# Idle matmuls of 512 columns, two memsets for eleven, and a branch placed three products later

## The chip, the cores and the metric

One Trainium2 chip, one of its cores. The metric is the device time of one execution in microseconds, the median of the runs.

## The reference

The kernel computes two layers in one launch. The first is an attention whose keys and values are mixed between blocks by a matrix that five Sinkhorn steps make from `sort_net`; the second is a gated feed-forward layer with a spatial product over the 768 tokens.

```python
# P: (4, 8, 8, 8), five times: exp(P - max), divided by row sums, then by column sums
k_sorted = einsum('bhij,bhjcd->bhicd', P, k_blocks)      # 8 blocks of 96 tokens
v_sorted = einsum('bhij,bhjcd->bhicd', P, v_blocks)
attn = softmax(q_block @ k_sorted_block.T / 8)           # within each block
x = (attn @ v_sorted_block)                              # -> (4, 768, 512)

h = maximum(x @ w_in, 0)                                 # (4, 768, 1024)
u, v = h[..., :512], h[..., 512:]
v_n = (v - mean(v)) / sqrt(var(v) + 1e-6)
v_s = einsum('ts,bsd->btd', w_spatial, v_n) + b_spatial[None, :, None]
out = (u * v_s) @ w_out                                  # (4, 768, 512) float32
```

q, k and v are (4, 8, 768, 64) float32. The kernel multiplies in bfloat16 and sums in float32.

## The kernel before

The order of all work is written by hand. The string `ORDER` is a list of short items, and each names a function `u_...` with its arguments: `SC:2:1:3:1` is the score product with its exp in PSUM tile 2 for batch 1, head pair 3, half 1. The items are issued in this order; each engine takes its own instructions from the list and waits only for the semaphores that the recording layer derives from the tiles it reads and writes. There are four PSUM tiles of two banks, `ps0` to `ps3`, and each item names the one that it uses.

The work goes over the four batches. For each one: q is turned (`QT`, `QQ`), k is mixed and turned in one product (`KT`), v is mixed (`VT` and `VB` for the first batch, `VM` and `VC` later), scores and exps per half (`SC`), product with v and division (`AT`), turning of x (`XT`, `XD`), the second half of `w_in` (`VP`), statistics (`ST`, `LN`, `LA`), the first half (`UP`), the spatial product (`SP`, `GT`) and the output product (`OP`, `OE`, `OS`). The batches overlap in the list. Loads of q, k, v and the weights are issued on GpSimd (`L`), most stores on SyncE.

The items that the change and the prediction speak of:

- `CO` (`u_CO`) clears `warm`, `eps` and `ones` and then the pads of the exp buffers `ex` (five) and of the turned k buffers `kt` (six), all on VectorE. The pads are the 32 columns behind the data, which 128-column weight loads read beyond a block of 96.
- `DM` (`u_DM`, L226) issues matmuls on the zero tile `warm` whose results nobody reads; they keep TensorE busy at the start. `DM:0:12:256` is twelve of 256 columns into `ps0`. Six groups stand before the first mixing of k: three of twelve by 256, then three of six by 512.
- `SK` (L238 to L251) is a Sinkhorn step, an exp on ScalarE and seven short VectorE operations. Its first exp waits for the load of `sort_net`.
- `QT` (L314) turns q of the first batch on TensorE after ScalarE has cast it (`QC`).
- `KT` and `VT` (L383) mix k and v of the first batch; `VT` needs the load `v_in`.
- `SH` (L666) is the spatial product of the last batch in pieces of 512 and 256 tokens, with the addition on VectorE (L672), and `GH` (L679) the gating.
- `OH` (L686) is an output product of the last batch, four matmuls over a token tile and a column range; `OI` copies it from PSUM (L115 on ScalarE, L117 on VectorE), and `OJ` stores it (L698). There are eight such products: `OH:1:3:2` and `OH:2:3:3` of 512 columns, `OH:0:3:4` and `OH:3:3:5` of 256, `OH:2:3:5` of 256, `OH:1:3:1` of 512, `OH:3:3:4` of 256, and last `OH:2:3:0` of 512.
- `IF` is the place of a branch (L794). A flag that the kernel has computed on the way (`CK`, `CF`, `LF`) says whether the fast arithmetic without maxima stayed in range; each engine reads it into a register. The items behind `IF` are the usual branch, and the alternative does the whole computation again in a safe way. Every engine resolves the branch in its own sequencer. `BH` marks the branch as likely taken for TensorE, VectorE and ScalarE. Before the change `IF` stands ahead of all eight output products.

Of the kernel before, what the change touches and what calls it, by code (L numbers as in the profile page):

```python
# [16 lines left out]

ORDER = """
IV:0 CO S0 SK:0 SK:1 LH:S:0 L:q:0:4:8 L:k:0:0:8 L:v:0:0:8 SK:2 IV:2 ID MA L:v:1:0:8 MC QC:A:1 SK:3 L:k:1:0:8 MB QC:A:0
DM:0:12:256 L:q:1:0:8 DM:2:12:256 DM:1:12:256 QT:3:A:0:1 SK:4 QT:2:A:0:3 DM:0:6:512 DM:3:6:512 L:wv QT:1:A:0:0  # L20
QT:2:A:0:2 PR:0 P0:0:2 L:wu P0:6:8 P0:2:4 DM:3:6:512 P0:4:6 PC:D KT:1:D:0:1 PD:1:4:8 KT:3:A:0:0 L:wsb L:wsa KT:0:D:0:3
KT:2:A:0:2 IV:1 L:v:2:0:8 VT:1:A:0:0 VT:3:D:0:1 PD:1:0:4 SC:0:0:0:0 SC:2:0:0:1 VB:1:D:0:0 L:k:2:0:8 VB:3:D:0:1
SC:0:0:1:0 VT:1:A:0:2 AT:2:0:0:0 VT:3:A:0:3 PD:2:4:8 AT:0:0:1:0 L:q:2:0:8 VM:1:A:1:0 VB:2:D:0:2 SC:3:0:1:1
XT:0:D:0:0:0 AT:1:0:0:1 SC:2:0:2:0 VM:3:A:1:3 VB:0:D:0:3 PD:2:0:4 SC:1:0:2:1 AT:2:0:2:0 KT:3:D:1:1 KT:0:D:1:2
SC:1:0:3:0 VM:2:A:1:1 SC:3:0:3:1 AT:1:0:1:1 KT:2:A:1:3 KT:0:A:1:0 AT:3:0:3:0 VM:1:A:1:2 PD:3:4:8 QQ:2:D:1:0
XT:3:D:0:1:0 L:k:3:0:8 AT:0:0:3:1 XT:1:A:0:0:2 QQ:2:A:1:2 AT:3:0:2:1 VP:1:A:0:0:1 XT:0:D:0:1:2 ST:0:1 VP:2:D:0:2
ST:0:0 SC:0:1:1:1 SC:3:1:2:1 L:q:3:0:8 VC:1:4:8 VP:1:D:0:4:5 SC:2:1:3:1 ST:0:4 ST:0:5 SC:3:1:3:0 VP:0:A:0:3 SC:2:1:0:1
ST:0:2 UP:1:A:0:1:1 AT:0:1:1:1 L:v:3:0:8 SC:3:1:0:0 ST:0:3 UP:2:A:0:0:0 AT:0:1:3:1 AT:1:1:2:1 LN:0:0:6 UP:3:A:0:0:1
AT:0:1:0:1 LA:0:5 WW:2:A:0 WW:1:D:4 XT:3:A:1:1:2 UP:0:A:0:1:0 LA:0:2 VC:1:0:4 AT:2:1:0:0 VM:1:A:2:1 BI WW:3:D:2
SC:0:1:2:0 VM:2:A:2:2 XT:1:D:1:1:0 LA:0:0 BH LA:0:4 LA:0:1 LA:0:3 VM:3:A:2:0 SC:0:1:1:0 VP:1:A:1:4:5 AT:2:1:3:0  # L30
AT:0:1:1:0 ST:1:5 SP:3:0:2 AT:0:1:2:0 L:wo SP:1:0:0 VM:2:D:2:3 SP:0:0:1 VC:2:4:8 XT:3:D:1:0:2 XT:1:A:1:0:0 VC:2:0:4
QQ:2:D:2:0 KT:0:A:2:1 KT:3:D:2:0 GT:D:0:0 QQ:1:D:2:2 KT:2:A:2:2 KT:0:A:2:3 PD:3:0:4 GT:P:0:2 VP:3:A:1:0:1 SC:1:2:0:1
SC:2:2:0:0 SP:0:0:3 ST:1:4 SC:3:2:2:1 SC:1:2:1:1 ST:1:1 VP:2:A:1:2:3 KT:3:D:3:2 QQ:0:D:3:0 ST:1:2 SC:1:2:3:0
UP:2:A:1:1:0 AT:0:2:0:1 GT:P:0:3 KT:3:A:3:0 ST:1:3 QQ:1:D:3:2 SC:0:2:3:1 AT:2:2:2:1 UP:3:D:1:0:1 VM:1:A:3:3
UP:0:A:1:0:0 AT:2:2:3:1 UP:3:A:1:1:1 GT:P:0:1 ST:1:0 LN:1:0:6 AT:2:2:1:1 AT:0:2:3:0 XD:2:1 LA:1:4 OP:1:0:0 AT:2:2:0:0
OE:A:0:0 OP:0:0:2 SC:2:2:2:0 LA:1:2 LA:1:5 OE:D:0:2 SC:1:2:1:0 LA:1:1 LA:1:0 LA:1:3 OP:3:0:4 AT:1:2:1:0 AT:0:2:2:0
SP:2:1:2 VM:0:D:3:1 VM:1:D:3:0 OE:A:0:4 VP:3:D:2:4:5 KT:0:A:3:1 KT:2:D:3:3 SP:1:1:3 VM:0:A:3:2 GT:D:1:3 OS:0:0 ST:2:4
SP:3:1:1 SC:2:3:3:1 SC:1:3:1:1 XD:2:0 OS:0:2 GT:D:1:2 ST:2:5 SP:0:1:0 VC:3:4:8 SC:3:3:2:1 SC:2:3:0:1 UP:1:D:2:1:0
GT:D:1:1 VC:3:0:4 VP:3:A:2:2:3 AT:1:3:3:1 GT:P:1:0 VP:2:A:2:0:1 ST:2:3 AT:1:3:2:1 AT:3:3:1:1 UP:0:A:2:1:1 OP:1:1:0
ST:2:0 ST:2:1 ST:2:2 OE:A:1:0 AT:2:3:0:1 LN:2:0:6 LA:2:1 UP:0:D:2:0:0 SC:1:3:0:0 LA:2:3 SC:3:3:1:0 LA:2:2 LA:2:5  # L40
LA:2:0 OP:2:1:4 AT:1:3:0:0 AT:3:3:1:0 XD:3:1 OE:A:1:4 OP:0:1:2 LA:2:4 SC:1:3:3:0 OE:D:1:2 SC:3:3:2:0 SP:2:2:2
AT:1:3:2:0 UP:0:A:2:0:1 AT:3:3:3:0 CK VP:2:A:3:4:5 GT:D:2:2 OS:1:2 SP:1:2:1 ST:3:5 OS:1:4 XD:3:0 SP:3:2:3 SP:2:2:0
ST:3:4 CF:3 GT:D:2:1 GT:P:2:3 UP:0:A:3:1:0 VP:2:D:3:2:3 VP:3:A:3:0:1 ST:3:0 ST:3:1 ST:3:2 UP:2:A:3:0:1 GT:P:2:0 LF
OP:1:2:2 ST:3:3 OE:A:2:2 LN:3:0:6 OP:0:2:0 LA:3:4 LA:3:5 OS:2:2 OE:A:2:0 UP:3:D:3:1:1 LA:3:2 LA:3:0 OP:2:2:4 LA:3:3
OE:A:2:4 LA:3:1 OS:2:4 UP:0:A:3:0:0 SH:1:3:3:0 GH:P:3:3:0 SH:2:3:0:0 GH:D:3:0:0 SH:0:3:1:0 SH:2:3:2:0 SH:3:3:1:1
GH:P:3:1:0 SH:1:3:0:1 GH:P:3:2:0 OS:1:0 GH:P:3:1:1 SH:2:3:3:1 SH:3:3:2:1 OS:2:0 GH:P:3:0:1 GH:D:3:2:1 GH:D:3:3:1
OS:0:4 IF OH:1:3:2:0:512:0:4 OH:2:3:3:0:512:0:4 OH:0:3:4:0:256:0:4 OI:A:3:2:0:512 OI:A:3:3:0:512 OH:3:3:5:0:256:0:4
OI:D:3:4:0:256 OI:D:3:5:0:256 OJ:3:2:0:512:S OJ:3:3:0:512:S OJ:3:4:0:256:S OJ:3:5:0:256:A OH:2:3:5:256:512:0:4
OH:1:3:1:0:512:0:4 OH:3:3:4:256:512:0:4 OI:D:3:5:256:512 OI:A:3:1:0:512 OJ:3:5:256:512:S OI:A:3:4:256:512
OJ:3:4:256:512:S OJ:3:1:0:512:A OH:2:3:0:0:512:0:4 OI:A:3:0:0:512 OJ:3:0:0:512:S  # L50
"""


# [12 lines left out]
def kernel(  # L66
# [131 lines left out]
    def u_CO():  # L198
        nc.vector.memset(warm, 0.0)  # L199
        nc.vector.memset(eps_tile, 1e-6)  # L200
        nc.vector.memset(ones, 1.0)
        for n in range(NE):
            nc.vector.memset(ex[n][:, 2 * NI * BLK:], 0.0)
        for n in range(NK):
            nc.vector.memset(kt[n][:, S:], 0.0)
# [622 lines left out]
```

## Time and profile before

| what | value |
|---|---|
| listed runs | 157.03, 157.03 and 158.32 us, median 157.03 us |
| profiled execution | 158.39 us, its span 156.6 us |
| granted TensorE clock in it | 0.989 of full speed (mean) |
| busy share of the span | TensorE 95%, VectorE 77%, ScalarE 52%, GpSimd 24% |
| chain that ended last | TensorE 84%, DMA 9%, ScalarE 2% |
| start of the branch | ScalarE 140.0, SyncE 142.9, TensorE 146.3, GpSimd 147.0, VectorE 148.4 us |

Rows are read as follows. A timeline row is: start, time, engine, line, operation, tile written and tile read, shape, count, and in brackets the idle time before it with what ended it. Rows of a chain are: start, time, engine and line. "q" behind an engine's name means its sequencer (ACTq), and PEld is TensorE's weight load, whose sequencer is PEldq. A matmul's time is from its start to its modelled end, so that neighbours overlap.

### The profile page before, as it was taken

To read this page: it belongs to the slowest core of one execution; us is meant where nothing else is said; L and a number is where in the kernel's file an instruction comes from. 1 tells how busy PE (TensorE), PEld (TensorE's weight loads), DVE (VectorE), ACT (ScalarE), POOL (GpSimd) and SP (SyncE) were. 2 spreads that over 40 slices of the span, in tenths; PEclk is the share of its full clock that TensorE was granted. 3 is DMA by queue.
4 is the path that set the end of the run, shared out by engine and by line. 5 is a ranking of instruction groups with operands and counts; after the bars stand their busy time and mean duration, and the time that the engine had idled before them with its cause. 6 is when DMAs were issued, how large, how long until landed. Compare 5 with 4: busy or idle time off the path is not lost.

```text
span 156.6 us, 4025 instructions
## 1 busy us (share of the span) xinstructions
PE 148.7 (95%) x1683; PEld 92.8 (59%) x1683; DVE 120.4 (77%) x270; ACT 81.8 (52%) x112; POOL 36.9 (24%) x43
## 2 busy tenths in 40 slices
...
PEclk9999879999999999999999999999999999999999
...
GB/s 80 262 203 205 203 205 205 206 211 234 255 240 205 204 205 204 230 208 4 0 4 234 10 229 43 153 14 4 100 107 199 66 0 0 110 51 375 148 218 186
DMA packets 27653, 23.57 MB, mean 151 GB/s; under 512 B 7280, under 2 KB 24688, under 8 KB 27632
## 3 DMA queue, kind: packets, MB, share of 16 engines
...
q10 hardware_dynamic: 288, 0.39, 0.7%
q8 instruction: 14, 0.23, 0.5%
...
HBM read 24.78 MB, written 6.29 MB: 198 GB/s over the span
## 4 chain that ended last, share of the span: by engine, by line
PE 84%; DMA 9%; ACT 2%; POOL 1%; DVE 1%; issue 1%; ACTq 0%; POOLq 0%
PE ps L609 15%; PE ps L597 14%; PE ps L554 14%; PE ps L636 10%; DMA v_in<-in_v_dram 9%; PE ps L488 5%; PE ps L666 5%; PE ps L442 4%; PE ps L383 4%; PE ps L686 3%; PE ps L314 3%; PE ps L410 2%; PE ps L518 2%; PE ps L401 1%; PE ps L531 1%; POOL q_in L169 1%
## 5 line engine op out<-in xcount | busy, mean ns | idle before, releaser
L447 ACT ACTIVATE ex<-ps 96x768 bf16<-96x768 f32 x32 | 24.8, 805 | 9.5 <-PE ps L442 9.5
L626 POOL TENSOR_TENSOR gt<-z,u_sb 128x768 bf16<-128x768 f32 x6 | 9.8, 1640 | 81.0 <-DVE z L615 61.2
L609 PE MATMUL ps<-wspT,v_sb 128*128 128x384 bf16 x144 | 25.1, 326 | 0.0
L597 PE MATMUL ps<-xT,w_in_sb 128*128 128x384 bf16 x128 | 23.5, 326 | 0.0
L496 DVE TENSOR_TENSOR x_sb<-ps,rec_all 96x512 bf16<-96x512 f32 x32 | 22.0, 686 | 1.1
L554 PE MATMUL ps<-w_in_sb,xT 128*128 128x512 bf16 x96 | 22.7, 380 | 0.0
L609 PEld LDWEIGHTS <-v_sb 128*128 128x128 bf16 x144 | 13.5, 98 | 8.9
L571 DVE BATCH_NORM_STATS2 stats<-v_sb 128x6 f32<-128x512 bf16 x24 | 16.3, 678 | 2.0 <-ACT v_sb L121 1.5
L115 ACT COPY o_sb<-ps 128x1024 f32<-128x1024 f32 (+2 forms) x12 | 9.7, 816 | 15.2 <-PE ps L686 10.2
L636 PE MATMUL ps<-w_out_sb,gt 128*128 128x512 bf16 x72 | 16.9, 379 | 0.0
L615 DVE TENSOR_TENSOR z<-ps,b_bc 128x768 f32<-128x768 f32 x12 | 11.4, 952 | 7.0 <-PE ps L609 6.8
L121 ACT ACTIVATE u_sb<-ps 128x768 bf16<-128x768 f32 x12 | 9.7, 810 | 13.1 <-PE ps L597 13.0
L597 PEld LDWEIGHTS <-w_in_sb 128*128 128x128 bf16 x128 | 11.6, 98 | 7.4
L554 PEld LDWEIGHTS <-xT 128*128 128x128 bf16 x96 | 8.7, 98 | 9.3
L121 ACT ACTIVATE v_sb<-ps 128x1024 bf16<-128x1024 f32 (+1 forms) x9 | 8.8, 976 | 8.7 <-PE ps L554 8.7
L488 PEld LDWEIGHTS <-ex 96*128 96x128 bf16 x256 | 10.7, 98 | 3.6 <-issue 0.2
L488 PE MATMUL ps<-vb,ex 96*128 96x65 bf16 x256 | 12.3, 195 | 0.0
L226 PE MATMUL ps<-warm 128*128 128x256 bf16 (+1 forms) x54 | 10.0, 353 | 1.3 <-DVE warm L199 1.3
L636 PEld LDWEIGHTS <-gt 128*128 128x128 bf16 x72 | 6.7, 98 | 7.2
L115 ACT CAST kt<-ps 128x768 bf16<-128x768 f32 x9 | 6.9, 800 | 6.5 <-PE ps L383 6.5
L442 PE MATMUL ps<-qT,kt 64*128 64x96 bf16 x256 | 9.4, 206 | 0.5 <-DVE kt L117 0.4
L442 PEld LDWEIGHTS <-kt 64*128 64x128 bf16 x256 | 6.3, 95 | 5.8 <-issue 3.9
...
## 6 DMA issues: line engine op xcount, KB each, us to landing
...
```

The lines of the kernel that those rows point to most:

```text
L115: nc.scalar.copy(out=out, in_=in_)
L121: nc.scalar.activation(out=out, in_=in_, func=AF.Relu)
L442: nc.tensor.matmul(t[:, hh, 0:HW].rearrange("p (g x) -> p g x", g=G)[:, :, ii * TB:(ii + 1) * TB], lhsT=kT[rows, i * BLK:i * BLK + 128], r ...
L447: nc.scalar.activation(out=e_tile(b, hp, ih).rearrange("p h (x g) -> p h x g", g=G), in_=t[0:BLK, :, 0:HW].rearrange("p h (g x) -> p h x g ...
L488: nc.tensor.matmul(t[:, hh, ii * VW:ii * VW + D + 1], lhsT=e[:, c:c + 128], rhs=vb[b % 2][:, ih * NI + ii, 2 * hp + hh, 0:D + 1], start=Tr ...
L496: nc.vector.tensor_mul(out=x_sb[:, hp].rearrange("p i (h d) -> p h i d", h=2), in0=tv[:, :, :, 0:D], in1=_raw_ap(rec, 0, [rec.ap[0], [NI, ...
L554: nc.tensor.matmul(t[:, x, :], lhsT=st["xT", b][:, n // 3, kc, (n % 3) * 128:(n % 3 + 1) * 128], rhs=w_in_sb[:, kc, DH:DFF], start=(kc == ...
L571: nc.vector.bn_stats(out=stats, in_=st["v_sb", b, n])
L597: nc.tensor.matmul(t[:, x, 0:HW], lhsT=w_in_sb[:, kc, mc * 128:(mc + 1) * 128], rhs=st["xT", b][:, ih, kc, :], start=(kc == 0), stop=(kc = ...
L609: nc.tensor.matmul(t[:, x, 0:HW], lhsT=st["v_sb", b, n][:, mc * 128:(mc + 1) * 128], rhs=wspT[:, 3 * x:3 * x + 3, n, :], start=(n == 0), s ...
L615: nc.vector.tensor_add(out=z.rearrange("p (x c) -> p x c", x=2), in0=t[:, :, 0:HW], in1=b_bc.rearrange("p (x c) -> p x c", x=2),)
L636: nc.tensor.matmul(t[:, x, :], lhsT=st["gt", b, mc][:, (n0 + x) * 128:(n0 + x + 1) * 128], rhs=w_out_sb[:, mc, :], start=(mc == 0), stop=( ...
```

## The change

Three edits. The first three groups of idle matmuls become six of 512 columns, so that all six groups are alike. The five `ex` buffers become slices of one tile `ex_all`, the six `kt` buffers slices of `kt_all`, and the pads of each are cleared by one memset over all slices. In `ORDER`, the first three output products `OH`, with their two copies on ScalarE and one on VectorE, stand ahead of `IF`; their stores stay behind it. The order among them is the same except that `OI:D:3:4` now comes before `OH:3:3:5`, on another engine than that one.

```diff
-DM:0:12:256 L:q:1:0:8 DM:2:12:256 DM:1:12:256 QT:3:A:0:1 SK:4 QT:2:A:0:3 DM:0:6:512 DM:3:6:512 L:wv QT:1:A:0:0
+DM:0:6:512 L:q:1:0:8 DM:2:6:512 DM:1:6:512 QT:3:A:0:1 SK:4 QT:2:A:0:3 DM:0:6:512 DM:3:6:512 L:wv QT:1:A:0:0 QT:2:A:0:2
...
-OS:0:4 IF OH:1:3:2:0:512:0:4 OH:2:3:3:0:512:0:4 OH:0:3:4:0:256:0:4 OI:A:3:2:0:512 OI:A:3:3:0:512 OH:3:3:5:0:256:0:4
-OI:D:3:4:0:256 OI:D:3:5:0:256 OJ:3:2:0:512:S OJ:3:3:0:512:S OJ:3:4:0:256:S OJ:3:5:0:256:A OH:2:3:5:256:512:0:4
+GH:P:3:1:1 SH:2:3:3:1 SH:3:3:2:1 OS:2:0 GH:P:3:0:1 GH:D:3:2:1 GH:D:3:3:1 OS:0:4 OH:1:3:2:0:512:0:4 OH:2:3:3:0:512:0:4
+OH:0:3:4:0:256:0:4 OI:A:3:2:0:512 OI:A:3:3:0:512 OI:D:3:4:0:256 IF OH:3:3:5:0:256:0:4 OI:D:3:5:0:256 OJ:3:2:0:512:S
+OJ:3:3:0:512:S OJ:3:4:0:256:S OJ:3:5:0:256:A OH:2:3:5:256:512:0:4 OH:1:3:1:0:512:0:4 OH:3:3:4:256:512:0:4
...
-    ex = [const.tile([BLK, 2 * NI * BLK + 32], BF16, name=f"ex{n}") for n in range(NE)]
-    kt = [const.tile([128, S + 32], BF16, name=f"kt{n}") for n in range(NK)]
+    ex_all = const.tile([BLK, NE, 2 * NI * BLK + 32], BF16, name="ex_all")
+    kt_all = const.tile([128, NK, S + 32], BF16, name="kt_all")
+    ex = [ex_all[:, n] for n in range(NE)]
+    kt = [kt_all[:, n] for n in range(NK)]
...
-        for n in range(NE):
-            nc.vector.memset(ex[n][:, 2 * NI * BLK:], 0.0)
-        for n in range(NK):
-            nc.vector.memset(kt[n][:, S:], 0.0)
+        nc.vector.memset(ex_all[:, :, 2 * NI * BLK:], 0.0)
+        nc.vector.memset(kt_all[:, :, S:], 0.0)
```

More of the change, by code (lines that the diff above doesn't have):

```diff
@@ L19 @@
 IV:0 CO S0 SK:0 SK:1 LH:S:0 L:q:0:4:8 L:k:0:0:8 L:v:0:0:8 SK:2 IV:2 ID MA L:v:1:0:8 MC QC:A:1 SK:3 L:k:1:0:8 MB QC:A:0
-DM:0:12:256 L:q:1:0:8 DM:2:12:256 DM:1:12:256 QT:3:A:0:1 SK:4 QT:2:A:0:3 DM:0:6:512 DM:3:6:512 L:wv QT:1:A:0:0
-QT:2:A:0:2 PR:0 P0:0:2 L:wu P0:6:8 P0:2:4 DM:3:6:512 P0:4:6 PC:D KT:1:D:0:1 PD:1:4:8 KT:3:A:0:0 L:wsb L:wsa KT:0:D:0:3
-KT:2:A:0:2 IV:1 L:v:2:0:8 VT:1:A:0:0 VT:3:D:0:1 PD:1:0:4 SC:0:0:0:0 SC:2:0:0:1 VB:1:D:0:0 L:k:2:0:8 VB:3:D:0:1
-SC:0:0:1:0 VT:1:A:0:2 AT:2:0:0:0 VT:3:A:0:3 PD:2:4:8 AT:0:0:1:0 L:q:2:0:8 VM:1:A:1:0 VB:2:D:0:2 SC:3:0:1:1
@@ L24 @@
[L24 to L43, printed above, removed]
@@ L49 @@
-OH:1:3:1:0:512:0:4 OH:3:3:4:256:512:0:4 OI:D:3:5:256:512 OI:A:3:1:0:512 OJ:3:5:256:512:S OI:A:3:4:256:512
-OJ:3:4:256:512:S OJ:3:1:0:512:A OH:2:3:0:0:512:0:4 OI:A:3:0:0:512 OJ:3:0:0:512:S
+DM:0:6:512 L:q:1:0:8 DM:2:6:512 DM:1:6:512 QT:3:A:0:1 SK:4 QT:2:A:0:3 DM:0:6:512 DM:3:6:512 L:wv QT:1:A:0:0 QT:2:A:0:2
+PR:0 P0:0:2 L:wu P0:6:8 P0:2:4 DM:3:6:512 P0:4:6 PC:D KT:1:D:0:1 PD:1:4:8 KT:3:A:0:0 L:wsb L:wsa KT:0:D:0:3 KT:2:A:0:2
+IV:1 L:v:2:0:8 VT:1:A:0:0 VT:3:D:0:1 PD:1:0:4 SC:0:0:0:0 SC:2:0:0:1 VB:1:D:0:0 L:k:2:0:8 VB:3:D:0:1 SC:0:0:1:0
@@ new lines @@
+VT:1:A:0:2 AT:2:0:0:0 VT:3:A:0:3 PD:2:4:8 AT:0:0:1:0 L:q:2:0:8 VM:1:A:1:0 VB:2:D:0:2 SC:3:0:1:1 XT:0:D:0:0:0
+AT:1:0:0:1 SC:2:0:2:0 VM:3:A:1:3 VB:0:D:0:3 PD:2:0:4 SC:1:0:2:1 AT:2:0:2:0 KT:3:D:1:1 KT:0:D:1:2 SC:1:0:3:0 VM:2:A:1:1
+SC:3:0:3:1 AT:1:0:1:1 KT:2:A:1:3 KT:0:A:1:0 AT:3:0:3:0 VM:1:A:1:2 PD:3:4:8 QQ:2:D:1:0 XT:3:D:0:1:0 L:k:3:0:8
+AT:0:0:3:1 XT:1:A:0:0:2 QQ:2:A:1:2 AT:3:0:2:1 VP:1:A:0:0:1 XT:0:D:0:1:2 ST:0:1 VP:2:D:0:2 ST:0:0 SC:0:1:1:1 SC:3:1:2:1
+L:q:3:0:8 VC:1:4:8 VP:1:D:0:4:5 SC:2:1:3:1 ST:0:4 ST:0:5 SC:3:1:3:0 VP:0:A:0:3 SC:2:1:0:1 ST:0:2 UP:1:A:0:1:1
@@ new lines @@
+AT:0:1:1:1 L:v:3:0:8 SC:3:1:0:0 ST:0:3 UP:2:A:0:0:0 AT:0:1:3:1 AT:1:1:2:1 LN:0:0:6 UP:3:A:0:0:1 AT:0:1:0:1 LA:0:5
+WW:2:A:0 WW:1:D:4 XT:3:A:1:1:2 UP:0:A:0:1:0 LA:0:2 VC:1:0:4 AT:2:1:0:0 VM:1:A:2:1 BI WW:3:D:2 SC:0:1:2:0 VM:2:A:2:2
+XT:1:D:1:1:0 LA:0:0 BH LA:0:4 LA:0:1 LA:0:3 VM:3:A:2:0 SC:0:1:1:0 VP:1:A:1:4:5 AT:2:1:3:0 AT:0:1:1:0 ST:1:5 SP:3:0:2
+AT:0:1:2:0 L:wo SP:1:0:0 VM:2:D:2:3 SP:0:0:1 VC:2:4:8 XT:3:D:1:0:2 XT:1:A:1:0:0 VC:2:0:4 QQ:2:D:2:0 KT:0:A:2:1
+KT:3:D:2:0 GT:D:0:0 QQ:1:D:2:2 KT:2:A:2:2 KT:0:A:2:3 PD:3:0:4 GT:P:0:2 VP:3:A:1:0:1 SC:1:2:0:1 SC:2:2:0:0 SP:0:0:3
@@ new lines @@
+ST:1:4 SC:3:2:2:1 SC:1:2:1:1 ST:1:1 VP:2:A:1:2:3 KT:3:D:3:2 QQ:0:D:3:0 ST:1:2 SC:1:2:3:0 UP:2:A:1:1:0 AT:0:2:0:1
+GT:P:0:3 KT:3:A:3:0 ST:1:3 QQ:1:D:3:2 SC:0:2:3:1 AT:2:2:2:1 UP:3:D:1:0:1 VM:1:A:3:3 UP:0:A:1:0:0 AT:2:2:3:1
+UP:3:A:1:1:1 GT:P:0:1 ST:1:0 LN:1:0:6 AT:2:2:1:1 AT:0:2:3:0 XD:2:1 LA:1:4 OP:1:0:0 AT:2:2:0:0 OE:A:0:0 OP:0:0:2
+SC:2:2:2:0 LA:1:2 LA:1:5 OE:D:0:2 SC:1:2:1:0 LA:1:1 LA:1:0 LA:1:3 OP:3:0:4 AT:1:2:1:0 AT:0:2:2:0 SP:2:1:2 VM:0:D:3:1
+VM:1:D:3:0 OE:A:0:4 VP:3:D:2:4:5 KT:0:A:3:1 KT:2:D:3:3 SP:1:1:3 VM:0:A:3:2 GT:D:1:3 OS:0:0 ST:2:4 SP:3:1:1 SC:2:3:3:1
```

13 lines of the change are left out of this document (10 added, 3 removed).

## The prediction

> **What bounds the kernel now.** I read the page first, then the chain that ended last, then the start, the clock and the end as timelines.
>
> ```profile
> span 156.6 us, 4025 instructions
> PE 148.7 (95%) x1683; PEld 92.8 (59%) x1683; DVE 120.4 (77%) x270; ACT 81.8 (52%) x112; POOL 36.9 (24%) x43
> ...
> PEclk9999879999999999999999999999999999999999
> ...
> PE 84%; DMA 9%; ACT 2%; POOL 1%; DVE 1%; issue 1%; ACTq 0%; POOLq 0%
> ```
>
> TensorE (PE) holds 84% of the chain; the one other large link is a DMA. The chain in order of time, first its head, then its end (start us, us, what):
>
> ```profile
> 1.27 0.93 POOL q_in L169
> 2.20 0.88 POOL k_in L169
> 3.08 13.68 DMA v_in<-in_v_dram
> ...
> 16.80 0.55 PE ps L383 x12
> ```
>
> ```profile
> 139.97 7.80 PE ps L666 x48
> 147.77 5.21 PE ps L686 x32
> 152.99 0.02 issue
> 153.01 0.58 ACT o_sb L115
> ```
>
> Up to 16.8 us the kernel waits for the first v. What goes on before that counts only if it delays this DMA or takes PE past 16.8. The end is the reverse: the spatial products (L666) run without a gap into the 32 output matmuls (L686), then one ScalarE (ACT) copy and the last store. An edit at the end counts only if it changes when the last L686 matmul is done.
>
> **Change, part one: 18 idle matmuls of 512 columns for 36 of 256.** The start, from the timeline:
>
> ```profile
> 1.19 0.17 DVE L203 MEMSET ex<- 96x16 uint32 x5
> ...
> 1.28 5.78 PE L226 MATMUL ps<-warm 128*128 128x256 bf16 x36 [1.28 <-DVE warm L199]
> 1.30 0.19 DVE L205 MEMSET kt<- 128x16 uint32 x6
> ...
> 2.67 0.21 DVE L239 TENSOR_REDUCE first<-p_all 32x8 f32<-32x64 f32 x1 [1.17 <-ACT p_all L238]
> ...
> 7.45 0.86 PE L314 MATMUL ps<-ident,q_in 128*64 128x128 bf16 x24 [0.39 <-ACT q_in L115]
> ...
> 8.24 2.76 PE L226 MATMUL ps<-warm 128*128 128x512 bf16 x12
> ...
> 16.80 0.86 PE L383 MATMUL ps<-pd,v_in 128*64 128x128 bf16 x24 [1.85 <-DMA v_in<-in_v_dram]
> ```
>
> The 36 come in two paces; the first row below is the stretch to 4.6 us, the second the one from 4.9 (as min/median/max ns, first and last start us):
>
> ```profile
> L226 PE MATMUL ps<-warm x16: 393/421/421, 1.3 to 4.4; 128*128 128x256 bf16 x16
> ...
> L226 PE MATMUL ps<-warm x20: 272/273/317, 4.7 to 6.8; 128*128 128x256 bf16 x20
> ```
>
> 16 matmuls in 3.4 us are 0.21 us each, the later 20 are 2.1/19 = 0.11 us apart. At 512 columns the fast pace is in the x12 row: 2.76 us less one duration of about 0.38, over 11, is 0.22 us. No row has 512 columns at the slow pace; twice 0.21 is 0.42. So about 8 of the 18 fill the 3.4 us to 4.7, the other 10 take 2.2 us, and the group ends near 7.0 where it ended at 7.06. The number of columns is the same, and the columns set the time. Bounds for the unseen pace: all 18 at the fast pace end at about 5.2, all 18 at 0.42 end at about 8.9. What hides either: the q transposes start at 7.45, when ACT has cast q, so an earlier end is worth nothing; 1.5 us later would still lie inside the 1.85 us that PE waits for v at 16.80. Without that cover the bounds would be -1.9 and +1.8 us. I take 0.
>
> **Part two: eleven memsets become two, and the pads lie in one tile each.** VectorE (DVE) runs them from 1.19 to 1.49 and then waits 1.17 us for the first exp until 2.67. Two larger ones cost at least one small one each (72 ns by the x6 group, 0.19 us with overlap) and, by the 256-column memset of warm, at most 0.27 us each: from -0.2 to +0.3 us of DVE time, all under that wait. I take 0. Uncovered, it would be that range. What could leak is the issue of q on GpSimd (POOL), 0.93 us during the memsets against 0.88 for k: up to 0.05 us earlier for v, so -0.05 to 0 on the path. With ex and kt each in one tile a copy might be made to wait for readers of another slice. In the built program it is not: outside the end, every instruction waits for the same engines at the same places as before.
>
> **Part three: the branch moves behind three output products and their copies.** The sequencers' side of the branch (ns min/median/max, first and last start us), and what each does next:
>
> ```profile
> L794 ACTq COMPARE_BRANCH  x1: 68/68/68, 140.0 to 140.0; - x1
> ...
> L794 PEldq COMPARE_BRANCH  x1: 481/481/481, 146.3 to 146.3; - x1
> ...
> L794 DVEq COMPARE_BRANCH  x1: 84/84/84, 148.4 to 148.4; - x1
> ```
>
> ```profile
> L115 ACTq EVENT_SEMAPHORE  x5: 17/38/8164, 140.5 to 152.7; - x5
> ```
>
> ```profile
> L686 PEldq EVENT_SEMAPHORE  x1: 51/51/51, 147.0 to 147.0; - x1
> ```
>
> ```profile
> L117 DVEq EVENT_SEMAPHORE  x5: 21/50/933, 149.0 to 150.4; - x5
> ```
>
> From branch to next instruction: ACT 0.5, PE 0.7, DVE 0.6 us. The timeline around it:
>
> ```profile
> 147.61 5.36 PE L686 MATMUL ps<-w_out_sb,gt 128*128 128x512 bf16 x32
> ...
> 149.54 0.58 ACT L115 COPY o_sb<-ps 128x512 f32<-128x512 f32 x1 [0.23 <-PE ps L686]
> 150.03 1.24 DVE L117 COPY o_sb<-ps 128x256 f32<-128x256 f32 x3 [0.93 <-PE ps L686]
> 150.87 0.39 ACTq L698 DMA_DIRECT2D out_dram<-o_sb  x1
> 151.71 0.86 ACT L115 COPY o_sb<-ps 128x512 f32<-128x512 f32 x2 [1.59 <-PE ps L686]
> ```
>
> PE: its sequencer branched at 146.3, while the array's next output matmul began at 147.61. It ran 1.3 us ahead, the branch took 0.7 of it, and the chain shows no gap. The move saves PE nothing. Afterwards the twelve matmuls before the branch (8 of 512, 4 of 256 columns) hold at least as many instructions of lead and longer ones, at least 1.3 us again. Cost 0; bounds 0 to 0.7 if the lead were gone.
>
> ACT: two copies now stand before its branch. It branches after starting the second at 149.54 and goes on at about 150.05; its next work is the issue of the fourth product's store at 150.87, which waits for DVE. Hidden with 0.8 us over.
>
> DVE loses its cover. Before, the 0.6 us lay in its 0.93 us wait for PE. Now the branch comes behind the copy at 150.03, goes on at about 150.63, passes two semaphore instructions (50 ns each, with gaps 0.15 us), and starts the second copy near 150.8, not 150.41. Queued behind are that copy and the third, 0.44 us apart: they end near 151.2 and 151.7. Who waits: the seventh and eighth products, which reuse those PSUM tiles, and ACT's store of the second copy. Counting products of 0.86 us (512 columns) and 0.44 (256) from 147.61, these two start at 151.51 and 151.95, as the stretches show (PE busy first):
>
> ```profile
> 151.51:151.95 0.44, 0.44 (x6) 0.39 (x5) 1.00 1.03 352
> 151.95:152.97 1.02, 1.02 (x6) 0.29 (x3) 1.00 0.91 312
> ```
>
> Both have some 0.3 us left. ACT's store is issued by 151.6, before its copy at 151.71. So 0.4 us is lost on DVE and 0 at the end. Bounds: below, a gain of 0, since the products are back to back; above, the branch may last until 0.9 us before anything moves, and each further microsecond is one at the end.
>
> **The sum.** Head -0.05 to 0, idle matmuls 0, memsets 0, branch 0: the profiled time of 158.39 us (span 156.6 and 1.8 around it) stays at about 158.35. That execution is not like the median. The clock stretches (PE busy and count, weight loads, DVE, ACT, POOL, granted clock):
>
> ```profile
> 14.90:16.80 1.90, 0.05 (x3) 0.01 (x2) 0.91 (x2) 0.92 (x2) 1.90 (x4) 1.00 1.30 197
> 16.80:18.30 1.50, 1.39 (x41) 1.15 (x42) 0.60 (x1) 0.94 (x2) 1.00 (x2) 1.00 1.32 205
> 18.30:21.70 3.40, 3.40 (x44) 2.88 (x44) 1.73 (x3) 2.43 (x4) 1.97 (x2) 0.51 1.32 204
> 21.70:25.10 3.40, 3.40 (x69) 2.64 (x68) 3.13 (x8) 3.07 (x5) 1.44 (x2) 0.98 1.31 204
> ```
>
> After PE's idle 1.9 us the clock was granted at half for 3.4 us, with 44 matmuls where the next 3.4 us hold 69: a loss of about 3.4 x (1 - 44/69) = 1.2 us. The profiled 158.39 is 1.36 above the median of 157.03 and beside the highest run, 158.32. So I read the 157.03 runs as those without this stretch, and forecast their like: 157.0 us, own range 156.7 to 157.3.
>
> **Rivals.** *A, the half-clock stretch falls into the median.* The idle time that calls it stays, and one listed run in three looks like it. Against it: nothing in the change lengthens that wait, and two of three runs were free. Time: 157.03 + 1.2 to 1.36, about 158.3. [...]
>
> *B, the other side: DVE's branch is late.* Place: between its first and second copy of the last outputs. It decides from 0.9 us of branch. For it: its cover is gone, and the three sequencers already differ by 0.2. If its next code had to be brought in on demand, I price that like a small transfer here:
>
> ```profile
> DMA to landing us min/median/max: 2.0/2.1/2.2
> ```
>
> Then 0.6 + 2.1 = 2.7 us of branch, 1.8 beyond the margin: 158.8. Against it: all branches seen took 0.5 to 0.7. [...]
>
> *C, faster: outside the profiled execution PE does lose the branch's 0.7 us,* and the change gives it back: 156.3; if the median of before also holds the half-clock stretch and that goes, 155.1. Against it: the chain's back-to-back 147.77 us. That the change does not do what it says is in the forecast itself: as many idle columns, cleared pads that nobody waited for.
>
> **How the numbers follow.** Forecast 0.58, A 0.15, B 0.14, C 0.13. A measurement of this kernel tells about 1% (1.6 us) from no change. Slower by more: most of B (0.10), A with a few tenths on top (0.05), 0.02 unexplained. Faster by more: half of C (0.07) and 0.02. Within: 0.74. The range 156.3 to 158.6 takes in A and C's first price and leaves out about 0.1 on each side.
>
> **What would show it.** Right: idle matmuls of 512 columns ending by about 7.0 and the transposes again at 7.4; PE waiting 1.8 us or so for v; L686 following L666 without a gap; DVE's second copy some 0.4 us behind its first one's end; the store after the last copy as before. Wrong: a gap of PE before the seventh or eighth product (B), a second stretch of half clock, exps or k copies waiting longer than before, or an L686 chain that begins earlier against L666 (C).

## The result, and the profile after

The change costs time. The runs of the changed kernel have a median of 157.9 us (157.42 to 158.25, 20 runs) against 157.03 us of the kernel before (156.26 to 158.32, 20 runs): ratio 1.0059, 95% interval 1.0044 to 1.0075. I had forecast 157.0 us and no difference. The profiled execution after took 157.98 us and is typical of its runs. Ratios here and below leave out runs over 1.5% above the fastest of the same kernel, which are two runs of the third edit alone.

The page of the kernel after: span and instructions, busy times, the granted clock in 40 slices, the chain by engine.

```profile
span 156.2 us, 3979 instructions
...
PE 148.5 (95%) x1665; PEld 90.0 (58%) x1665; DVE 120.2 (77%) x261; ACT 81.7 (52%) x112; POOL 36.8 (24%) x43
...
PEclk9999999999999999999999999999999999999996
...
PE 90%; ACT 3%; DVE 2%; issue 2%; ACTq 1%; DVEq 0%
```

The DMA link of 9% is gone from the chain, and so is the dip of the clock. ACT and its queue have come in. The chain's last pieces, from two stretches of the same view (start us, us, what):

```profile
138.26 7.80 PE ps L666 x48
146.06 2.18 PE ps L686 x12
149.83 1.57 ACTq L698
...
152.00 0.39 ACT o_sb L115
...
152.57 0.59 ACT o_sb L115
```

L666 starts 1.71 us earlier than in the profile of before (139.97), and yet the span is only 0.4 us shorter: from there to the end it is 17.9 us (156.2 - 138.26) instead of 16.6 (156.6 - 139.97). The chain leaves the output matmuls after twelve of 32 and goes through the issue of a store on ACT. So something is won in the head, and more is lost in the tail.

**The head.** The timeline after:

```profile
13.94 1.53 PE L383 MATMUL ps<-pd,k_in 128*64 128x128 bf16 x48
...
15.52 0.86 PE L383 MATMUL ps<-pd,v_in 128*64 128x128 bf16 x24
```

PE goes from k to v with no wait, where it had waited 1.85 us for v to land: v landed at 16.75 us before and at 15.37 after. With that wait went the half-clock stretch: the mean granted clock was 0.991 or higher in all 20 runs, while seven of the 35 runs of before in the first batch below had 0.984 to 0.989, and these were the ones of 158.1 to 158.4 us. The DMA queues from 13 to 16 us show what else went (queue and kind: packets, MB, share of 16 engines), first before, then after:

```profile
q0 software_dynamic: 787, 0.59, 129.1%
q8 instruction: 1, 0.02, 2.0%
q14 instruction: 1, 0.01, 0.7%
```

```profile
q0 software_dynamic: 811, 0.61, 131.5%
```

q8 brings blocks of 16 KB (14 in each of these two profiles), q14 blocks of 8 KB. I read those of q8 as PE's code and those of q14 as that of other engines: below, the idle matmuls alone move q8's block from here (to 17.03 us) and leave q14's, and the memsets alone move q14's (to 18.23 us) and leave q8's. Before, their records stand at 14.72 and 14.21 us, in the middle of the load of v. After, with 36 instructions fewer on PE (18 matmuls, 18 weight loads) and nine memsets fewer on DVE ahead of them, they come at 17.53 and 18.24.

**The tail.** The stores of the last batch (ns min/median/max, first and last start us), before and after, the last row with the time to landing; the landing row of before stands in the prediction.

```profile
L698 SPq DMA_DIRECT2D out_dram<-o_sb x6: 332/338/402, 149.3 to 153.6; - x6
L698 ACTq DMA_DIRECT2D out_dram<-o_sb x2: 339/364/389, 150.9 to 152.3; - x2
```

```profile
L698 SPq DMA_DIRECT2D out_dram<-o_sb x6: 332/348/1985, 147.6 to 153.2; - x6
L698 ACTq DMA_DIRECT2D out_dram<-o_sb x2: 338/1112/1885, 149.5 to 152.1; - x2
...
DMA to landing us min/median/max: 2.0/3.2/4.4
```

One issue on SP and one on ACT now take 1.9 us and more instead of 0.4. ACT's copies stand behind its own. The first row here is the rest of the output matmuls:

```profile
146.54 4.72 PE L686 MATMUL ps<-w_out_sb,gt 128*128 128x512 bf16 x29
...
148.26 0.42 DVE L117 COPY o_sb<-ps 128x256 f32<-128x256 f32 x1 [0.87 <-PE ps L686]
149.06 0.75 DVE L117 COPY o_sb<-ps 128x256 f32<-128x256 f32 x2 [0.38 <-PE ps L686]
149.52 1.89 ACTq L698 DMA_DIRECT2D out_dram<-o_sb  x1
151.52 0.86 ACT L115 COPY o_sb<-ps 128x512 f32<-128x512 f32 x2 [3.12 <-PE ps L686]
...
152.57 0.59 ACT L115 COPY o_sb<-ps 128x512 f32<-128x512 f32 x1 [0.19 <-ACT o_sb L115]
```

The last output matmul ends at 151.26 and the last copy at 153.16, 1.90 us behind; before it was 152.97 and 153.60, 0.63 us. The bracket "<-PE" of the copy at 151.52 misleads: its matmuls were long done, and the row above it shows what ACT was doing. Again code is on its way at that time. PE's 16 KB block that follows its branch begins at 148.69 and takes 1.81 us where the one before takes 0.96, and two 8 KB blocks follow at 149.32 and 149.56.

### The profile page after: what moved, and what is told of

Its sections match the earlier page's. It is cut to its first block, busy times and chain, and to the rows that moved or that the text cites. A ratio compares the mean times of both kernels' runs of the same rounds, so it can differ in the third digit from the quotient of the medians.

```text
span 156.2 us, 3979 instructions
## 1 busy us (share of the span) xinstructions
PE 148.5 (95%) x1665; PEld 90.0 (58%) x1665; DVE 120.2 (77%) x261; ACT 81.7 (52%) x112; POOL 36.8 (24%) x43
## 4 chain that ended last, share of the span: by engine, by line
PE 90%; ACT 3%; DVE 2%; issue 2%; ACTq 1%; DVEq 0%
PE ps L609 15%; PE ps L597 14%; PE ps L554 14%; PE ps L636 10%; PE ps L226 7%; PE ps L488 5%; PE ps L666 5%; PE ps L442 4%; PE ps L383 4%; PE ps L314 4%; PE ps L410 2%; PE ps L518 2%; PE ps L686 1%; PE ps L531 1%; ACTq L698 1%
## 5 line engine op out<-in xcount | busy, mean ns | idle before, releaser
L447 ACT ACTIVATE ex_all<-ps 96x768 bf16<-96x768 f32 x32 | 24.8, 807 | 8.6 <-PE ps L442 8.6
L488 PEld LDWEIGHTS <-ex_all 96*128 96x128 bf16 x256 | 10.6, 97 | 4.2 <-issue 0.6
L488 PE MATMUL ps<-vb,ex_all 96*128 96x65 bf16 x256 | 12.2, 193 | 0.5 <-issue 0.5
L226 PE MATMUL ps<-warm 128*128 128x512 bf16 x36 | 11.0, 470 | 1.3 <-DVE warm L201 1.3
L115 ACT CAST kt_all<-ps 128x768 bf16<-128x768 f32 x9 | 6.9, 800 | 6.5 <-PE ps L383 6.5
L442 PE MATMUL ps<-qT,kt_all 64*128 64x96 bf16 x256 | 9.3, 204 | 0.5 <-DVE kt_all L117 0.4
L495 DVE RECIPROCAL rec_all<-ps 96x8 f32<-96x8 f32 x32 | 6.3, 195 | 4.3 <-PE ps L488 4.0
```

Of the source, the lines that this page charges most:

```text
L115: nc.scalar.copy(out=out, in_=in_)
L226: nc.tensor.matmul(t[:, 0, 0:int(w)], lhsT=warm[:, 0:128], rhs=warm[:, 0:int(w)], start=True, stop=True)
L442: nc.tensor.matmul(t[:, hh, 0:HW].rearrange("p (g x) -> p g x", g=G)[:, :, ii * TB:(ii + 1) * TB], lhsT=kT[rows, i * BLK:i * BLK + 128], r ...
L447: nc.scalar.activation(out=e_tile(b, hp, ih).rearrange("p h (x g) -> p h x g", g=G), in_=t[0:BLK, :, 0:HW].rearrange("p h (g x) -> p h x g ...
L488: nc.tensor.matmul(t[:, hh, ii * VW:ii * VW + D + 1], lhsT=e[:, c:c + 128], rhs=vb[b % 2][:, ih * NI + ii, 2 * hp + hh, 0:D + 1], start=Tr ...
```

## The experiments

Each run was measured beside the kernel before on the same chip, whose medians were 157.1 us (batch of the first four), 156.85 (the second four), 156.99 (the third four) and 156.94 (the last two). Its runs fall mostly into three groups, near 156.25, 157.05 and 158.3 us; the third is missing in the batch of the second four. Theories carry numbers of their own in each expectation. Mine was that code, loaded in blocks by DMA, decides both ends; the rivals were a later start (the idle matmuls) and DVE's later second copy (rival B of the prediction).

### The edits one by one

**The third edit alone.** The kernel of before with this order behind OS:0:4:

```diff
-IF OH:1:3:2 OH:2:3:3 OH:0:3:4 OI:A:3:2 OI:A:3:3 OH:3:3:5 OI:D:3:4 OI:D:3:5:0
+OH:1:3:2 OH:2:3:3 OH:0:3:4 OI:A:3:2 OI:A:3:3 OI:D:3:4 IF OH:3:3:5 OI:D:3:5:0
```

> Before with the third edit alone: three products and their copies ahead of the branch; idle matmuls and memsets as before. Theory T1 (code loads among the stores): about 1.25 us after a branch TensorE loads its next 16 KB of code, ScalarE and VectorE 8 KB; after the move these fall among the first output stores and hold up one DMA engine, so a store's issue takes some 1.9 us instead of 0.4 and the last copies come late: 0.6 to 1.3 us slower than before, a store issue of over 1 us in the trace. Theory T2 (the start): 0 within 0.2 us. Theory T3 (VectorE's branch late, rival B of the prediction): 0.3 to 1 us slower, with TensorE idle before the seventh or eighth product and store issues near 0.4 us.

Measured: 158.28 us, ratio 1.008 (1.0037 to 1.0124), as theory 1 had it. The seven runs with a granted clock of 0.992 or more took 157.37 to 158.33 us, the five with 0.988 or 0.989, so with the half-clock stretch, 159.25 to 159.98. v is waited for as before, and the tail is that of the changed kernel: first the timeline at v, then the stores.

```profile
16.74 0.86 PE L382 MATMUL ps<-pd,v_in 128*64 128x128 bf16 x24 [1.72 <-DMA v_in<-in_v_dram]
```

```profile
L697 SPq DMA_DIRECT2D out_dram<-o_sb x6: 332/347/1731, 147.9 to 153.5; - x6
L697 ACTq DMA_DIRECT2D out_dram<-o_sb x2: 338/1088/1839, 149.9 to 152.5; - x2
```

PE's block after the branch came at 148.96 and took 1.65 us. The last copy ended 1.85 us behind the last matmul. So the loss at the end belongs to the third edit, and the half-clock stretch is still there without the first two.

**The first two edits alone,** the branch ahead of all products as before:

```diff
-DM:0:12:256 ... DM:2:12:256 DM:1:12:256
+DM:0:6:512 ... DM:2:6:512 DM:1:6:512
+(two memsets for eleven; IF stays behind OS:0:4)
```

> Before with the first two edits alone: idle matmuls of 512 columns and two memsets; the branch ahead of all products. T1: 0 within 0.3 us of before. T2 (the idle matmuls now stand on the chain and delay the start): 0.6 to 1.2 us slower. T3: 0.

Measured: 158.32 us, ratio 1.0094 (1.0062 to 1.0126), all runs within 158.12 to 158.68. The head is that of the changed kernel (v at 15.62 without a wait), no store issue takes over 0.41 us, and still it is slower. The loss is here:

```profile
L794 PEldq COMPARE_BRANCH  x1: 2862/2862/2862, 144.8 to 144.8; - x1
```

I had not thought of this at all: PE's branch takes 2.86 us instead of 0.48, though it and all that is around it are unchanged. The waits put PE's idle time on DVE's gating, which ended last by the profile:

```profile
PE ps L686 <- DVE gt L679: 1.6, 1, 1.6
```

The kernels below, in which the branch is short and PE does not idle there, show that it is the branch. None of my theories had this cause; theory 2's 0.6 to 1.2 us comes near the loss by luck.

**Each of the two alone.** The memset edit alone:

```diff
+ex_all, kt_all and two memsets; ORDER of before
```

> The memset edit alone: the changed kernel's two memsets and joined tiles with the order of work of before. Theory 1 (blocks of code): PE's code is as before, so its 16 KB load stays at 14.7 us, and only DVE's 8 KB load moves from 14.2 to about 18; v lands 0.2 to 0.5 us earlier (16.2 to 16.6); the end is as before, with a PE branch of 0.4 to 0.5 us and a last copy 0.63 us behind the last matmul: 156.4 to 157.1 us. Rival (joining the tiles makes readers wait): over 157.4 us, with longer waits of exps or turned k.

Measured: 156.23 us (156.09 to 157.06), ratio 0.9983 (0.9961 to 1.0005), the fastest kernel of the study by its median, though not told from before. Its runs too fall near 156.15 and 157.0 us; the group near 158.3 is missing, as it is in the runs of before beside it. The idle matmuls alone:

```diff
-DM:0:12:256 ... DM:2:12:256 DM:1:12:256
+DM:0:6:512 ... DM:2:6:512 DM:1:6:512
```

> The idle matmul edit alone: 18 of 512 columns for 36 of 256 in the kernel of before. Theory 1 (blocks of code): PE's 16 KB load moves from 14.7 to about 17.5 us, DVE's 8 KB load stays at 14.2; v lands 0.7 to 1.2 us earlier (15.6 to 16.1); q transposes 0.4 to 0.6 us later than before; PE's branch takes 2.5 to 3 us, since the block that holds its target is asked for only then; 157.9 to 158.5 us. Rival (the slow pair of the first two edits is due to the memsets): PE's branch 0.5 us and 156.6 to 157.1 us.

Measured: 158.25 us (158.11 to 158.6), ratio 1.0098 (1.0073 to 1.0123). PE's wait for v (us in total, times, longest) and its branch with the idle matmuls alone:

```profile
PE ps L383 <- DMA v_in<-in_v_dram: 1.0, 1, 1.0
```

```profile
L794 PEldq COMPARE_BRANCH  x1: 2862/2862/2862, 144.4 to 144.4; - x1
```

With the memsets alone, the timeline from k to v, the branch, and the chain's last long pieces:

```profile
13.90 1.53 PE L383 MATMUL ps<-pd,k_in 128*64 128x128 bf16 x48
...
15.48 0.86 PE L383 MATMUL ps<-pd,v_in 128*64 128x128 bf16 x24
```

```profile
L794 PEldq COMPARE_BRANCH  x1: 392/392/392, 144.1 to 144.1; - x1
```

```profile
137.69 7.80 PE ps L666 x48
145.50 5.21 PE ps L686 x32
```

The slow branch comes with the fewer idle matmuls. Each edit moves the block of one engine out of the load of v: with the memsets alone DVE's comes at 18.23 and PE's stays at 14.96; with the idle matmuls alone PE's comes at 17.03 and DVE's stays at 14.23. PE then waits not at all, or 1.0 us, against 1.6 to 1.85 with both blocks in the way. The landing of v is the cleaner measure, since the wait also depends on when PE is done with k (it waits 0.3 to 0.5 us in five kernels with neither block there). v landed at 16.67 to 16.75 us in the four kernels with both blocks (five traces), at 15.89 with DVE's alone, at 15.31 with PE's alone, and at 15.31 to 15.53 in the nine with neither. So the landing goes with where the blocks lie, but PE's block costs only together with DVE's; how 8 and 16 KB hold up a load of 768 KB by so much is open. My sizes were too small for the memsets (PE on v at 15.48, not 16.2 to 16.6, and a median below my 156.4 to 157.1) and right for the idle matmuls, except that the q transposes came no later (7.44).

### The place of the branch in PE's code

The remaining kernels of this part move the branch by rows (a row is an instruction of PE in the built program). **Fewer idle matmuls,** to move it away from the edge of its block on the other side:

```diff
-DM:0:6:512 ... DM:2:6:512 DM:1:6:512
+DM:0:4:512 ... DM:2:4:512 DM:1:4:512
```

> The changed kernel with the branch back ahead of all output products, and the first three idle groups cut from six to four matmuls of 512 columns (six matmuls and their six weight loads fewer than in the run with the first two edits alone, so that PE's branch stands 12 instructions further ahead of the end of its block of code). Theory 1 (blocks of code, loaded by DMA, decide both ends): v lands by 15.6 us as in the changed kernel, the q transposes start near 7.5, PE's branch takes 0.4 to 0.5 us, no store issue takes over 1 us, the last copy ends 0.6 to 0.7 us after the last output matmul; 156.0 to 156.7 us, so 0.2 to 0.6% below before. Theory 2 (the slower start of the idle matmuls is the loss): PE's branch stays at 2.9 us as with the first two edits alone, and the time near 157.8 to 158.0.

Measured: 159.98 us, ratio 1.0211 (1.0186 to 1.0235): a clear miss. The branch became slower still (3.09 us). And 1.95 us of PE idle ahead of the q transposes were followed by a half-clock stretch, in which PE did 30 matmuls where the next 3.4 us hold 44 (us, PE busy and count, weight loads, DVE, ACT, POOL, granted clock):

```profile
7.50:10.90 3.40, 3.40 (x30) 1.85 (x27) 2.79 (x15) 2.60 (x5) 1.25 (x2) 0.50 1.31 204
10.90:14.30 3.40, 3.40 (x44) 1.90 (x43) 1.04 (x4) 1.27 (x2) 0.00 (x0) 1.00 1.32 204
```

Seven of the eight runs had a granted clock of 0.989 or less, and the eighth, 158.5 us, 0.998; so with fewer idle matmuls there the half clock comes in most runs. Rows taken away were the wrong direction, so I went the other way, with one and with two products ahead of the branch on the head of the changed kernel:

```diff
-OS:0:4 IF OH:1:3:2 ... OI:A:3:2
+OS:0:4 OH:1:3:2 OI:A:3:2 IF ...                       (one)
+OS:0:4 OH:1:3:2 OH:2:3:3 OI:A:3:2 OI:A:3:3 IF ...      (two)
```

> The first two edits, and one output product of 512 columns with its copy ahead of the branch instead of three (branch at row 3277; 3269 was slow, 3293 fast). Theory 1 (row of the branch): either below the edge, then the branch takes 2.8 to 3.0 us and some 0.8 us less of it shows than with the first two edits alone, 157.2 to 157.7 us; or above it, then 0.4 to 0.5 us and 155.9 to 156.5 us, with the last copy at most 1.0 us behind the last output matmul. Rival (a branch is fast when products are queued ahead of it): fast in any case, since 0.9 us of matmuls now covers it.

> As the run before, with two products of 512 columns and their copies ahead of the branch (row 3285). Theory 1 (row of the branch; code behind the branch in the way of the stores): slow below the edge (branch 2.8 to 3.0 us, of which 1.7 us is covered by the two products, 157.0 to 157.6 us); fast above it, with code arriving 0.4 to 0.5 us earlier against the stores than in the changed kernel: last copy 0.7 to 1.5 us behind the last output matmul, 156.2 to 157.4 us. Rival (the long store issues come from the third product's copy on DVE): no issue over 1 us, last copy 0.65 us behind, 156.0 to 156.4 us.

Measured: one 157.55 us, ratio 1.0032 (0.9999 to 1.0065); two 157.61 us, 1.004 (1.0009 to 1.0071). The branch took 2.00 and 1.52 us, so it was neither slow nor fast but in between, which neither theory had. PE idled 0.7 us before the second product in the first kernel and at no output product in the second, whose loss is in the tail: store issues of 1.05 and 1.91 us, and the last copy 1.56 us behind the last matmul, against 0.84 with one product. So the long issues do not come from the third product's copy on DVE, as the rival had it. The records of q8 tell why the branch is in between (the block is the last one of PE that began ahead of the branch's end; times in us):

| kernel | row | block begins | branch begins | takes | block's begin to branch's end |
|---|---|---|---|---|---|
| fewer idle matmuls | 3257 | 145.76 | 145.13 | 3.09 | 2.45 |
| idle matmuls alone | 3269 | 144.78 | 144.37 | 2.86 | 2.45 |
| first two edits | 3269 | 145.20 | 144.77 | 2.86 | 2.43 |
| one product | 3277 | 144.81 | 145.26 | 2.00 | 2.45 |
| two products | 3285 | 144.82 | 145.75 | 1.52 | 2.45 |
| changed kernel | 3293 | 145.08 | 147.43 | 0.48 | 2.83 |
| before | 3305 | 144.05 | 146.35 | 0.48 | 2.78 |

In the first five PE left the branch 2.43 to 2.45 us after a 16 KB block had begun to arrive. That block comes at one place of the program's rows, as I read it: 4.0 to 4.3 us after the first L666 matmul in kernels with the rows of before, 7.0 us after it in those with 36 rows fewer (7.2 with 48 fewer), whether the branch has begun by then or not. Before, the branch came 2.30 us behind the block's begin, and its own 0.48 us took it past the 2.45. So in those five the branch took 2.43 to 2.45 us less the time from the block's begin to its own. That the block holds the branch's target, as theory 1 of several expectations has it, no run shows; with one and with two products it began before the branch, so there the branch did not call for it.

**Rows put back.** The first two edits, and 18 idle matmuls of 16 columns (36 rows), once behind the first use of v and once in the wait for v:

```diff
+DM:1:18:16 ahead of AT:1:0:0:1        (behind)
+DM:1:18:16 ahead of VT:1:A:0:0        (in the wait)
```

> The first two edits alone (branch ahead of all output products, its place in PE's program row 3269), and 18 idle matmuls of 16 columns put in after the first v has been used, ahead of AT:1:0:0:1, so that PE's branch stands at row 3305 again, as before. Nothing near the branch changes. Theory 1 (the row at which the branch stands decides whether its target's code is there in time): the branch takes 0.4 to 0.5 us instead of 2.9, v lands by 15.6 us, the 18 tiny matmuls cost 0.5 to 1.0 us; 156.4 to 157.2 us. Rival (the branch is slow because of the memsets, the idle form or the time at which it comes): branch still 2.9 us, 158.8 to 159.4 us.

> The first two edits, the branch ahead of all output products, and 18 idle matmuls of 16 columns ahead of VT:1:A:0:0, where PE waits for the first v, so that the branch stands at row 3305. Theory 1 (row of the branch; v no longer behind the loads of code; idle matmuls in a wait cost nothing): PE's branch 0.4 to 0.5 us, no half-clock stretch in the head, no long store issue, PE starts on v by 15.8 us; 156.0 to 156.8 us in all runs. Rival (the tiny matmuls' cost is the rows themselves, wherever they stand): 157.4 to 157.7 us, as where they stood behind the first v.

Both branches are fast again, with nothing changed near them. The branch with the rows behind v; then, with the rows in the wait, the timeline there and the branch:

```profile
L794 PEldq COMPARE_BRANCH  x1: 482/482/482, 145.5 to 145.5; - x1
```

```profile
15.03 0.59 PE L226 MATMUL ps<-warm 128*128 128x16 bf16 x18
15.68 0.86 PE L383 MATMUL ps<-pd,v_in 128*64 128x128 bf16 x24
```

```profile
L794 PEldq COMPARE_BRANCH  x1: 481/481/481, 144.9 to 144.9; - x1
```

The block ahead of the branch now begins 2.29 and 2.49 us before it. So it is the branch's place in PE's rows that decides. The times: behind, 157.59 us, ratio 1.0064 (1.003 to 1.0098), 0.4 us over what I expected, with one run of 159.26 at a granted clock of 0.989; the first L666 matmul came at 138.99, 0.9 us later than in the changed kernel (138.09), of which the 18 matmuls are 0.60. In the wait, 156.87 us, 1.0001 (0.9974 to 1.0028), at the upper end of my range, with runs up to 157.65 outside it: the tiny matmuls cost less there, as theory 1 had it, but not nothing (first L666 matmul at 138.35). By the ratios to before it is 0.6% ahead of the changed kernel, and it ties with before.

### The stores

**One product ahead of the branch, in the kernel of before,** so with its head:

```diff
-OS:0:4 IF OH:1:3:2 ... OI:A:3:2
+OS:0:4 OH:1:3:2 OI:A:3:2 IF ...
```

> Before with only the first output product and its copy ahead of the branch. T1: TensorE's branch comes some 0.9 us later against the products, its code load ends about when the first store's packets start; 0 to 0.4 us slower, and less than with three products. T2: 0. T3: 0, since VectorE's branch keeps its cover.

Measured: 156.87 us, ratio 1.0003 (0.9955 to 1.0052), in two groups, 156.23 to 157.15 and 158.03 to 158.33. PE's block after the branch came at 147.05, ahead of the first store, and the one slower issue took 0.72 us; the last copy ended 0.84 us behind the last matmul. With the stores as they are, the last copy ends the later behind the last matmul the more products stand ahead of the branch: 0.84 us with one, 1.56 with two, 1.85 and 1.90 with three.

**The branch ahead of the spatial products,** so that all code behind it comes far from the stores:

```diff
-UP:0:A:3:0:0 SH:1:3:3:0 ... OS:0:4 IF
+UP:0:A:3:0:0 IF SH:1:3:3:0 ... OS:0:4
```

> Before with the branch ahead of the last batch's spatial products, some 9 us earlier for TensorE. T1: all code loads are over before the stores: -0.1 to +0.2 us, no store issue above 0.6 us. T2 and T3: 0 within 0.2 us. If the branch itself costs TensorE, 0.5 to 0.7 us slower.

Measured: 157.64 us, ratio 1.003 (0.9985 to 1.0076). No code arrives among the stores, and no issue takes over 0.41 us (first row); but ACT's copy into a reused buffer waited for a store (second), and the last copy ended 1.19 us behind the last matmul:

```profile
L697 SPq DMA_DIRECT2D out_dram<-o_sb x6: 332/338/413, 148.0 to 152.8; - x6
...
  ACT o_sb L114: 0.7, 1
```

By its median my time was a miss, in part for that reason, which lies in this kernel and not in the change; the interval takes in no difference at all.

**The fourth store on SP instead of ACT,** in the changed kernel:

```diff
-OJ:3:5:0:256:A
+OJ:3:5:0:256:S
```

> The changed kernel with the fourth store issued by SP instead of ACT, nothing else. Theory 1 (the code that PE, ACT and DVE load behind their branches holds up the stores, and ACT's copies stand behind its long store issue): ACT starts its copies on time, the last copy ends 0.6 to 1.0 us after the last output matmul instead of 1.9; the store issues on SP may be long; 156.7 to 157.3 us. Rival (DVE's later second copy is what holds ACT): ACT's last copies as late as in the changed kernel, 157.7 to 158.1 us.

Measured: 157.45 us (156.84 to 158.19), ratio to before 1.0043 (1.0017 to 1.007). ACT's copies no longer stand behind that issue; the SP issue is still long:

```profile
L697 SPq DMA_DIRECT2D out_dram<-o_sb x7: 332/383/1585, 147.3 to 152.1; - x7
L697 ACTq DMA_DIRECT2D out_dram<-o_sb x1: 946/946/946, 150.4 to 150.4; - x1
```

The last copy ended 1.03 us behind the last matmul instead of 1.90. DVE's second copy is as late as in the changed kernel (0.38 us idle), so DVE is not what holds ACT. By the ratios 0.25 us come back, with intervals that overlap, and less than I had expected (156.7 to 157.3); in the trace ACT's later issue of 0.95 us stands before the last copy.

**The first two stores issued later,** in the changed kernel:

```diff
-OJ:3:2 OJ:3:3 OJ:3:4:0:256 OJ:3:5:0:256 ... OJ:3:5:256:512
+OJ:3:4:0:256 OJ:3:5:0:256 ... OJ:3:5:256:512 OJ:3:2 OJ:3:3
```

> The changed kernel with the stores of its first two output copies (OJ:3:2 and OJ:3:3) issued behind OJ:3:5:256 instead of first, so that fewer bytes are on their way when PE, ACT and DVE load the code behind their branches. Theory 1 (the long issues come when a load of code and several stores meet): the two stores then first in line issue in 0.3 to 0.8 us instead of 1.9, ACT's copies start on time; 156.9 to 157.7 us. Rival (an issue is long whenever it falls within about 1.5 us of PE's load of code, with or without stores ahead): one or both still 1.5 to 2 us, 157.8 to 158.4 us.

Measured: 157.78 us, ratio to before 1.0063 (1.0044 to 1.0083). With one 128 KB store ahead instead of three stores, ACT's issue is still long:

```profile
149.34 1.64 ACTq L697 DMA_DIRECT2D out_dram<-o_sb  x1
151.11 0.86 ACT L114 COPY o_sb<-ps 128x512 f32<-128x512 f32 x2 [2.88 <-PE ps L685]
```

So the long issue does not need several stores ahead; my theory's version here fell, and the rival is nearer (157.78 lies between the two ranges). Over all traces, each issue of more than 1 us began while PE's 16 KB block behind the branch was on its way, and where that block was there before the second store none did. But not each issue within such a time was long (0.34 us at 148.19 with two products ahead of the branch, 0.35 at 149.08 with the idle matmuls alone). That the block in a DMA engine is what holds the issue, as the theory of the third edit alone had it, is my reading and not shown.

**The kernel before once more:**

> The kernel of before once more, for a second trace of it. Its runs come near 156.25, 157.05 or 158.3 us. Theory 1 (v's landing sets the lower two, the half-clock stretch the third): near 156.25 PE does not wait for v and there is no half-clock stretch; near 157.05 v lands at 16.7 to 16.8 us as in the first trace, without the stretch; near 158.3 as the first trace. Rival: v lands at 16.8 us in every execution, and the modes differ at the end.

Measured: 158.38 us, the first trace again (v at 16.72, half clock from 18.2 for 3.4 us, branch 0.48). It confirms the group near 158.3. What parts 156.25 from 157.05 no trace of before shows.

## Why the prediction was wrong, point by point

- **"outside the end, every instruction waits for the same engines at the same places as before", with idle matmuls and memsets at 0.** This step failed. The working priced the instructions' time, and that was nearly right: the groups of 512 columns cost nothing by themselves. In this execution the q transposes began at 7.96 instead of 7.45, and with the first two edits alone at 8.07, but in seven other kernels with these groups at 7.43 to 7.63, and with the memsets alone and groups of 256 at 7.93. It goes with the time at which the clock came up: 4.74 us before, 4.05 to 6.11 in those seven, 6.68 with the memsets alone, 6.77 after, 6.99 with the first two edits. What the working left out is that 45 instructions fewer move the times at which code is loaded, from 14.72 and 14.21 us to 17.53 and 18.24. PE's 1.8 us wait for v, which I called right if seen, is gone, and with it the half-clock stretch.
- **The price of that in the head.** Against kernels with the head of before and no stretch (L666 in the chain at 138.62 with one product ahead of the branch) the changed kernel is 0.36 us ahead (138.26); against the executions with the stretch 1.7. PE starts on v 1.2 us earlier than with one product ahead (15.52 against 16.73), so 0.85 us of that is gone again by L666; no run shows where.

```profile
138.62 7.80 PE ps L666 x48
```

- **PE's branch at 0.** Right for the changed kernel (482 ns, no gap), by a reason that I did not know. The lead, "at least 1.3 us again", was wrong in size: the branch began at 147.43, and the first output matmul behind it at 148.06, so the lead was 0.6 us and the branch used all but 0.15 of it. It was also the wrong quantity for how long the branch takes: in the first five kernels of the table above that went with the time since the block of code began to come, and here that time was 2.35 us. The two edits of the head alone cost 1.6 us of PE here, and the third edit, which moves the branch to a later row, takes that away. My bound "0 to 0.7 if the lead were gone" was far too low.
- **ACT's branch hidden, DVE's 0.4 late and harmless.** The branches took 68 and 84 ns, DVE idled 0.38 us between its copies. Right, and the products were back to back to 151.26.
- **"ACT's store is issued by 151.6, before its copy at 151.71."** This step failed as well, and it makes the result. I took 0.39 us for the issue, from the row of before, and it took 1.89; the copy started at 151.52 behind it, and one more copy after it. The term that I had as 0 is 1.27 us (1.90 - 0.63). What makes the issue long is not shown; that the third edit brings it is.
- **The sum, made anew:** -0.36 + 1.27 = +0.9 us on 157.03, the executions without stretch, gives 157.9, the median measured. That 157.03 is the time without the half-clock stretch held. The -0.36 rests on one execution of another kernel, since no trace of before without the stretch was taken.
- **The rivals.** A did not come: the stretch vanished. The idle time for v does not call the stretch each time: the third edit alone had 1.72 us of it and a granted clock of 0.998 in its trace. B named the right kind of cause, a long branch, but on the wrong engine and kernel, and that code brought in on demand makes it long no run shows: DVE's branch was short, and PE's was long in kernels other than the changed one. C failed in both halves: PE loses nothing at its branch in the executions without the stretch that were traced (one product ahead, the memsets alone), and the stretch that went was not in the median of before, whose runs near 157.05 had a granted clock of 0.996 or more.

That L666 begins 0.57 us later in the changed kernel (138.26) than with the memsets alone (137.69) stays open. PE idled 0.5 us ahead of L488 in the former with no releaser shown.
